# Attention on one core: normalising the last query block with a VectorE shuffle and a wide reciprocal

## Chip, cores, metric

One core of one Trainium2 chip (trn2). The metric is the time of one execution in microseconds (us) as the device reports it. The profile's span, from the first to the last instruction, is about 1.8 us shorter.

## The reference

Sixteen-head attention without mask on x of shape (1, 2048, 448), head size 28, with the QKV projection before it and the output projection after it:

```
qkv    = (x @ wqkv) reshaped to q, k, v of [B, 16, 2048, 28]
scores = einsum("bhqd,bhkd->bhqk", q, k) * 28 ** -0.5
p      = softmax(scores)
o      = einsum("bhqk,bhkd->bhqd", p, v)
out    = o (heads joined) @ wo
```

## The kernel before

Heads go in 4 groups of 4. Queries go in 4 blocks of 512. A window is one group with one block, so there are 16. In a window, the scores of each 128-key row go through an exponential, on ScalarE in tiles of 128x1024 or in a VectorE/GpSimd version, and then through PV matmuls into one PSUM bank `PO`. There each head has a strip of 32 partitions: 28 rows of unnormalised output, then row 28, the softmax denominator, because V is padded with ones. A scheduler in the kernel's Python interleaves all of this and fixes the order of instructions on each engine.

Fifteen windows get their denominators inverted in the background, by way of DMA. The last window has nothing left to hide behind. Before the change its tail was this (cut):

```python
# after key row 12 of 16: copy PO, gather the 13 rows' denominators by f32 matmuls
def partial_sums(pvop):
    ev = add(Op("DVE", 0.62, lambda: nc.vector.tensor_copy(out=OSB[...][:], in_=PO[:]), ...))
    chain_A(lambda tq: den_gather(PD[gbank[0]], ...), [ev], hold)       # lhsT = PO copy, rhs = sel
...
for j in range(NKT - NLAST, NKT):            # the last 3 key rows
    for i in range(HG):
        for tq in range(TPC):                # denominators: one-column matmuls, 48 in all
            nc.tensor.matmul(out=gb[:, col:col + 1], lhsT=pt[i][1]()[:, tq * P:(tq + 1) * P],
                             rhs=VA[g][:, 0, 0, Dh:Dh + 1], ...)
    for i in range(HG):                      # PV
        nc.tensor.matmul(out=PO[HP * st:HP * (st + 1), :], lhsT=VA[g][:, j, st, :], rhs=pt[i][1](), ...)
nc.vector.reciprocal(out=RT[:], in_=gb[:, 0:TPC * HG])      # 128 queries x 16 (4 heads x 4 tiles)
den_expand(0, nc.vector.tensor_copy); den_expand(1, nc.scalar.copy)
for hf in range(2):
    nc.vector.tensor_copy(out=OH[hf][:], in_=PO[:, hf * hw:(hf + 1) * hw])
acc(2, range(g))                             # output sums of the other three groups
for tq in range(TPC):                        # spread over the strips: f32 matmuls
    nc.tensor.matmul(out=spread[...], lhsT=RX[...], rhs=ident32[:], start=True, stop=True)
acc(3, range(g))
for hf in range(2):
    nc.vector.tensor_tensor(out=OTL[hf][:], in0=OH[hf][:], in1=spread[hf], op=ALU.mult)
    for tq in (2 * hf, 2 * hf + 1): acc(tq, (g,))
# ... two adds on VectorE, two casts on ScalarE, four output DMAs
```

The softmax here doesn't subtract the row's maximum and nothing guards it: scores larger than these inputs give would overflow.

## Time and profile before

| | before |
|---|---|
| median of 4 runs | 415.99 us (415.77 to 416.25) |
| profiled span | 414.2 us |
| ScalarE busy | 97% |
| end of the last exponential | 405.21 us |
| tail: from there to the end of the span | 9.0 us |

The page of the kernel before: the busy time of each engine, and the chain of waits followed back from the last instruction.

```profile
span 414.2 us, 7679 instructions
...
PE 366.8 (89%) x2679; PEld 124.9 (30%) x2679; DVE 395.1 (95%) x699; ACT 399.9 (97%) x439; POOL 224.9 (54%) x210
...
ACT 82%; PE 9%; issue 6%; DMA 1%; DVE 1%; SPq 0%; DVEq 0%
```

ScalarE bounds nearly the whole kernel. The 9% of TensorE does not measure the tail. Followed piece by piece (`--critical`), about 5 of these 36 us lie in the tail, 6.5 us before the first exponential and 24 us in the middle. The timeline of the tail (columns: start, duration, engine, source line, operation, output and inputs, count, idle time before it and what ended it):

```profile
403.92 1.29 ACT L934 ACTIVATE PTA_131<-PA_200 128x1024 bf16<-128x1024 f32 x1
...
404.79 0.34 PE L1069 MATMUL PD_201<-VA_110,PTA_142 128*128 128x1 bf16 x8
...
406.70 0.39 PE L1073 MATMUL PO<-PTA_131,VA_110 128*32 128x512 bf16 x2
406.80 0.26 DVE L1075 RECIPROCAL RT<-PD_201 128x16 f32<-128x16 f32 x1 [1.04 <-PE PD_201 L1069]
...
408.05 0.61 PE L1082 MATMUL PD_201<-ident_208,RX_214 128*128 128x128 f32 x4
...
408.69 0.42 DVE L1086 TENSOR_TENSOR OTL_220<-OH_211,PD_201 128x256 bf16<-128x256 f32 x1
...
409.44 0.54 PE L1062 MATMUL PA_199<-WO,OTL_220 128*128 128x448 bf16 x2
...
410.44 0.54 ACT L1093 CAST OUTF_218<-PA_199 128x448 bf16<-128x448 f32 x1
```

The last PV matmul (L1073) ends at 407.09, 1.9 us after the exponential that it needs, because TensorE still has gathers and one-column matmuls to do. VectorE's last multiply ends at 409.11. In the chain of waits of this tail, however, every piece from 402.90 to 409.99 is TensorE's, and VectorE's copies and multiplies fit in beside it. From the last PV on (start, duration, what):

```profile
407.09 0.67 PE PA_199 L1062 x3
407.76 0.44 PE PA_200 L1082 x4
408.21 0.45 PE PD_201 L1082 x4
408.65 0.57 PE PA_199 L1062 x3
```

### The profile page before, as it was taken

The numbers are of one execution on the slowest core, as the hardware profiler recorded it, in microseconds if no ns is written. First come the engines' busy times: TensorE is split into PE (matmuls) and PEld (weight loads), VectorE is DVE, ScalarE is ACT, GpSimd is POOL, SyncE is SP. The second block draws the span as 40 slices with busy tenths as digits, with TensorE's granted clock in tenths as the row PEclk, the third lists the DMA queues.
The fourth block names the chain that finished last, engine by engine and source line by source line (L and its number), as shares of the span: only waits on it lengthen the run. The fifth ranks groups of instructions, "written<-read, shape, count | busy, mean of one in ns | idle before, by whom it ended". The sixth has DMA issues, their size and how long they took to land.

```text
span 414.2 us, 7679 instructions
## 1 busy us (share of the span) xinstructions
PE 366.8 (89%) x2679; PEld 124.9 (30%) x2679; DVE 395.1 (95%) x699; ACT 399.9 (97%) x439; POOL 224.9 (54%) x210
## 2 busy tenths in 40 slices
PE   8988989898898889898897988889898988889995
PEld 5433222323232233323222222222322222222233
DVE  6899999999999999999999999999999999999974
ACT  4999999999999999999999999999999999999992
POOL 3155556474656547475555646456475656656440
PEclk9999999999999999999999999999999999999999
DMA  8410020202201011111400001010410101001012
GB/s 258 80 16 21 3 50 8 55 21 60 65 2 46 0 33 25 26 32 25 97 6 29 18 18 31 2 40 6 91 34 2 46 2 36 10 27 47 18 55 90
DMA packets 33414, 15.85 MB, mean 38 GB/s; under 512 B 26016, under 2 KB 30304, under 8 KB 33376
## 3 DMA queue, kind: packets, MB, share of 16 engines
q1 hardware_dynamic: 32304, 15.05, 14.5%
q8 instruction: 21, 0.34, 0.4%
q10 hardware_dynamic: 1072, 0.32, 0.3%
q14 instruction: 17, 0.14, 0.1%
HBM read 7.37 MB, written 1.96 MB: 23 GB/s over the span
## 4 chain that ended last, share of the span: by engine, by line
ACT 82%; PE 9%; issue 6%; DMA 1%; DVE 1%; SPq 0%; DVEq 0%
ACT PTA_131 L934 4%; ACT PTA_132 L934 4%; ACT PTA_133 L934 4%; ACT PTA_134 L934 4%; ACT PTA_145 L934 4%; ACT PTA_136 L934 4%; ACT PTA_135 L934 4%; ACT PTA_140 L934 4%; ACT PTA_144 L934 3%; ACT PTA_137 L934 3%; ACT PTA_141 L934 3%; ACT PTA_149 L934 3%; ACT PTA_148 L934 3%; ACT PTA_139 L934 3%; ACT PTA_138 L934 3%
## 5 line engine op out<-in xcount | busy, mean ns | idle before, releaser
L745 POOL TENSOR_TENSOR DG_181<-DV_175,DU_169 128x512 f16<-128x512 f16 x30 | 34.6, 1154 | 35.8 <-DVE DV_175 L742 35.6
L745 POOL TENSOR_TENSOR DG_182<-DV_176,DU_170 128x512 f16<-128x512 f16 x30 | 34.6, 1153 | 29.7 <-DVE DV_176 L742 29.1
L745 POOL TENSOR_TENSOR DG_184<-DV_178,DU_172 128x512 f16<-128x512 f16 x29 | 33.5, 1154 | 29.8 <-DVE DV_178 L742 28.5
L745 POOL TENSOR_TENSOR DG_185<-DV_179,DU_173 128x512 f16<-128x512 f16 x29 | 33.4, 1153 | 25.9 <-DVE DV_179 L742 25.8
L745 POOL TENSOR_TENSOR DG_186<-DV_180,DU_174 128x512 f16<-128x512 f16 x29 | 33.5, 1154 | 24.9 <-DVE DV_180 L742 24.7
L745 POOL TENSOR_TENSOR DG_183<-DV_177,DU_171 128x512 f16<-128x512 f16 x29 | 33.4, 1153 | 23.7 <-DVE DV_177 L742 23.6
L649 PEld LDWEIGHTS <-KB_1_94 64*128 64x128 bf16 x256 | 20.8, 93 | 48.2 <-issue 47.3
L649 PEld LDWEIGHTS <-KB_0_91 64*128 64x128 bf16 x256 | 20.5, 93 | 45.8 <-issue 42.1
L649 PEld LDWEIGHTS <-KB_1_92 64*128 64x128 bf16 x256 | 20.2, 93 | 45.8 <-issue 43.9
L649 PEld LDWEIGHTS <-KB_0_93 64*128 64x128 bf16 x256 | 20.5, 93 | 43.8 <-issue 42.7
L934 ACT ACTIVATE PTA_145<-PA_199 128x1024 bf16<-128x1024 f32 x18 | 22.6, 1254 | 0.0
L934 ACT ACTIVATE PTA_144<-PA_200 128x1024 bf16<-128x1024 f32 x18 | 22.5, 1250 | 0.0
L934 ACT ACTIVATE PTA_140<-PA_200 128x1024 bf16<-128x1024 f32 x18 | 22.5, 1249 | 0.0
L934 ACT ACTIVATE PTA_143<-PA_199 128x1024 bf16<-128x1024 f32 x18 | 22.4, 1247 | 0.0
L934 ACT ACTIVATE PTA_139<-PA_199 128x1024 bf16<-128x1024 f32 x18 | 22.4, 1246 | 0.0
L934 ACT ACTIVATE PTA_142<-PA_200 128x1024 bf16<-128x1024 f32 x18 | 22.4, 1242 | 0.0
L934 ACT ACTIVATE PTA_138<-PA_200 128x1024 bf16<-128x1024 f32 x18 | 22.3, 1241 | 0.0
L934 ACT ACTIVATE PTA_141<-PA_199 128x1024 bf16<-128x1024 f32 x18 | 22.3, 1240 | 0.0
L739 DVE TENSOR_SCALAR DU_171<-PD_203 128x512 f16<-128x512 uint16 x29 | 19.9, 685 | 1.0 <-PE PD_203 L649 0.7
L739 DVE TENSOR_SCALAR DU_172<-PD_201 128x512 f16<-128x512 uint16 x29 | 19.8, 682 | 0.9 <-PE PD_201 L649 0.9
L739 DVE TENSOR_SCALAR DU_169<-PD_201 128x512 f16<-128x512 uint16 x29 | 19.8, 684 | 0.5 <-PE PD_201 L649 0.5
L742 DVE SCALAR_TENSOR_TENSOR DV_178<-PD_201,DU_172 128x512 f16<-128x512 uint16 x29 | 19.9, 686 | 0.3
(618 smaller groups left out, 1515.5 us busy)
## 6 DMA issues: line engine op xcount, KB each, us to landing
RRB_195<-SCR_197 SPq DMA_DIRECT2D x8, 256.0 KB
RRB_196<-SCR_198 SPq DMA_DIRECT2D x7, 256.0 KB
KB_1_94<-KB_0_93 SPq DMA_DIRECT2D x4, 128.0 KB
XS_127<-in_x_dram SPq DMA_DIRECT2D x1, 448.0 KB
XS_128<-in_x_dram SPq DMA_DIRECT2D x1, 448.0 KB
XS_129<-in_x_dram SPq DMA_DIRECT2D x1, 448.0 KB
XS_130<-in_x_dram SPq DMA_DIRECT2D x1, 448.0 KB
out_dram<-XS_127 SPq DMA_DIRECT2D x1, 448.0 KB
```

The source lines that it names most:

```text
L649: nc.tensor.matmul(out=ap, lhsT=KB[g % 2][i // 2][a:a + 64, j * P:(j + 1) * P], rhs=QB[w % NQB][i // 2][a:a + 64, :], start=True, stop=Tru ...
L739: p1 = add(Op("DVE", P1, lambda: nc.vector.tensor_scalar(out=DU[b][:], in0=lo, scalar1=SIG / 65536, scalar2=SIG * (SS - 0.5), op0=ALU.mult ...
L742: p2 = add(Op("DVE", P1, lambda: nc.vector.scalar_tensor_tensor(out=DV[b][:], in0=lo, scalar=65536 * (SS - 0.5 + CE / C3), in1=DU[b][:], o ...
L745: gq = add(Op("POOL", PTT, lambda: nc.gpsimd.tensor_tensor(out=DG[b][:], in0=DV[b][:], in1=DU[b][:], op=ALU.mult), deps=[p2], prio=n, kind ...
L934: nc.scalar.activation(out=PTA[pslot.idx][:, 0:len(ns) * QW], in_=PA[s.idx][:, 0:len(ns) * QW], func=ACT.Exp, bias=ACT_BIAS, scale=ACT_SCALE)
```

## The change

The intent is to take the denominators' detour over TensorE out of the tail. A VectorE stream shuffle copies row 28 of each strip over the strip's 32 rows. A reciprocal and a multiply follow there, in two halves of 256 columns. The output sums of the other three groups are begun before the end, in whichever PSUM banks fall idle. Core of the diff (constants, set-up of `sel` and `ident32`, and the removed helpers cut):

```diff
-    SPLIT = {2: 4, 3: 2}
+    SPLIT = {2: (0, 1, 2, 3), 3: (2,)}
+    ACCQ = (0, 1, 3)
...
+    def late_sums():        # PE ops of low priority: three matmuls for each of 3 banks, once a bank is idle
+        ...
+                prev = add(Op("PE", 0.19, lambda tq=tq, gg=gg: nc.tensor.matmul(
+                    out=PD[late_acc[tq]][:, 0:D], lhsT=OT[gg][NQC - 1][:, tq * P:(tq + 1) * P], rhs=WO[:, gg, :],
+                    start=(gg == 0), stop=False), ...
...
-    for j in range(NKT - NLAST, NKT):   (one-column matmuls and PV of the last 3 rows; PV is now scheduled as usual)
-    nc.vector.reciprocal(out=RT[:], in_=gb[:, 0:TPC * HG])
-    den_expand(...) x2; tensor_copy OH x2; spread matmuls; acc(2), acc(3)
     for hf in range(2):
-        nc.vector.tensor_tensor(out=OTL[hf][:], in0=OH[hf][:], in1=spread[hf], op=ALU.mult)
+        cols = slice(hf * hw, (hf + 1) * hw)
+        nc.vector.stream_shuffle(out=DEN[hf][:], in_=PO[:, cols], mask=[Dh] * HP)
+        nc.vector.reciprocal(out=DEN[hf][:], in_=DEN[hf][:])
+        nc.vector.tensor_tensor(out=OTL[hf][:], in0=PO[:, cols], in1=DEN[hf][:], op=ALU.mult)
+        for tq in (2 * hf, 2 * hf + 1):
+            nc.tensor.matmul(out=fb[tq], lhsT=OTL[hf][:, ...], rhs=WO[:, g, :], start=(tq not in late_acc), stop=True)
...  # output tile 2 is added on VectorE, tiles 0, 1 and 3 are cast on ScalarE
```

More of the change, by code (lines that the diff above doesn't have):

```diff
@@ L108 @@
     JL = 6
+    JACC = 8
     DI = 2
-    WPE = 1
     PVM = 0.0
-    ADUR = 0.25
     PLD = 0.2
@@ L134 @@
     MG = 0.1
-    SPLIT = {2: 4, 3: 2}
+    SPLIT = {2: (0, 1, 2, 3), 3: (2,)}
+    ACCQ = (0, 1, 3)
+    ACCP = 2000
     PARTD = 60
@@ L173 @@
     DG = [sb([P, QW], F16, f"DG{i}") for i in range(NB)]
-    PARTL = [sb([P, D], F32, f"PARTL{i}") for i in range(2)]
+    PARTL = {tq: sb([P, D], F32, f"PARTL{tq}") for tq in SPLIT[NQC - 1]}
     OSB = [sb([P, QW], F32, f"OSB{i}") for i in range(2)]
@@ L189 @@
     zrow = sb([P, QW], BF16, "zrow")
-    ident32 = sb([P, P], F32, "ident32")
-    sel = sb([P, HG], F32, "sel")
-    OH = [sb([P, QW // 2], F32, f"OH{i}") for i in range(2)]
-    RT = sb([P, TPC * HG], F32, "RT")
-    RX = [sb([P, QW // 2], F32, f"RX{i}") for i in range(2)]
+    DEN = [sb([P, QW // 2], F32, f"DEN{i}") for i in range(2)]
     OUTF = [sb([P, D], BF16, f"OUTF{i}") for i in range(TPC)]
@@ L225 @@
                                 base=-(HP * i + Dh), pattern=[[0, 1]], channel_multiplier=1)
-    nc.gpsimd.memset(sel[:], 0.0)
-    for i in range(HG):
-        nc.gpsimd.affine_select(out=sel[:, i:i + 1], in_=sel[:, i:i + 1], compare_op=ALU.not_equal,
-                                fill=1.0, base=-(HP * i + Dh), pattern=[[0, 1]], channel_multiplier=1)
-    nc.gpsimd.memset(ident32[:], 0.0)
-    nc.gpsimd.affine_select(out=ident32[:], in_=ident32[:], compare_op=ALU.not_equal,
-                            fill=1.0, base=0, pattern=[[-1, P]], channel_multiplier=1)
     for g in range(G):
@@ L576 @@
     ot_done = {}
-    gbank = [None]
-    def hold(t):
-        free = [s for s in d_slots if s.free_at <= t + 1e-9]
-        if free:
-            free[0].free_at = 1e18
-            gbank[0] = free[0].idx
-        return bool(free)
     parts = {}
@@ L595, in task_part @@
         due = (12 + c) * WT - PARTD
-        for tq in range(n):
+        for tq in n:
             task = bank_task()
@@ L631 @@
     NW = G * NQC
-    NLAST = 3
-    NROW = NW * NKT - NLAST
+    NROW = NW * NKT
     rows = {}
@@ L655, in s_ready @@
                 and kmrep[(g, j // TPC, i)].done(t))
-    def chain_A(fn, deps, acq=None):
-        prev = None
-        for tq in range(TPC):
-            prev = add(Op("PE", ADUR, lambda tq=tq: fn(tq), deps=[prev] if prev else deps, prio=-5000 + tq, kind="A",
-                          lat=PLAT if tq == TPC - 1 else 0.0, acq=acq if tq == 0 else None))
-        return prev
-    def den_gather(dst, src, tqs=range(TPC)):
-        for tq in tqs:
-            nc.tensor.matmul(out=dst[:, tq * HG:(tq + 1) * HG], lhsT=src(tq), rhs=sel[:], start=(tq == 0), stop=True,
-                             skip_group_check=True)
@@ L670, in den_expand @@
-    def den_expand(hf, copy):
-        n = TPC * HG // 2
-        copy(out=RX[hf][:].rearrange("p (n e) -> p n e", e=HP),
-             in_=RT[:, hf * n:(hf + 1) * n].rearrange("p (n o) -> p n o", o=1).to_broadcast([P, n, HP]))
-    def den_spread(dst, tqs=range(TPC)):
-        for tq in tqs:
-            nc.tensor.matmul(out=dst[:, tq * P:(tq + 1) * P], lhsT=RX[tq // 2][:, (tq % 2) * P:(tq % 2 + 1) * P],
-                             rhs=ident32[:], start=True, stop=True)
-    def partial_sums(pvop):
-        ev = add(Op("DVE", 0.62, lambda: nc.vector.tensor_copy(out=OSB[(NW - 1) % 2][:], in_=PO[:]), deps=[pvop], prio=-5000))
-        chain_A(lambda tq: den_gather(PD[gbank[0]], lambda k: OSB[(NW - 1) % 2][:, k * P:(k + 1) * P], (tq,)), [ev], hold)
+    late_acc = {}
@@ new lines, in late_sums, with take, f @@
+    def late_sums():
+        def take(tq, n):
+            def f(t):
+                if pos[0] < NT - NTAIL or n and any(o.kind == "B" and o.acq is not None for o in static["PE"]):
+                    return False
+                free = [x for x in d_slots if x.free_at <= t + 1e-9]
+                if not free:
+                    return False
+                free[0].free_at = 1e18
+                late_acc[tq] = free[0].idx
+                return True
+            return f
+        prev = None
+        for n, tq in enumerate(ACCQ):
+            for gg in range(G - 1):
+                prev = add(Op("PE", 0.19, lambda tq=tq, gg=gg: nc.tensor.matmul(
+                    out=PD[late_acc[tq]][:, 0:D], lhsT=OT[gg][NQC - 1][:, tq * P:(tq + 1) * P], rhs=WO[:, gg, :],
+                    start=(gg == 0), stop=False), deps=([prev] if prev else []) + [ot_done[(g_, NQC - 1)] for g_ in range(G - 1)],
+                    prio=ACCP + tq + 0.1 * gg, kind="A", lat=0.0, acq=take(tq, n) if gg == 0 else None))
@@ L695, in finish_window @@
         ev.after = rel
-        if w >= NW - WPE:
-            ev.after = None
-            d1 = chain_A(lambda tq: den_gather(PO, lambda k: OSB[b][:, k * P:(k + 1) * P], (tq,)), [ev])
-            d2 = add(Op("DVE", 0.17, lambda: nc.vector.reciprocal(out=RT[:], in_=PO[:, 0:TPC * HG]), deps=[d1], prio=-5000))
-            d2a = [add(Op("DVE", 0.25, lambda hf=hf: den_expand(hf, nc.vector.tensor_copy), deps=[d2], prio=-5000)) for hf in range(2)]
-            d2b = chain_A(lambda tq: den_spread(PO, (tq,)), d2a)
-            d3 = add(Op("DVE", 0.62, lambda: nc.vector.tensor_tensor(out=OT[g][c][:], in0=OSB[b][:], in1=PO[:], op=ALU.mult),
-                        deps=[d2b], prio=-5000))
-            d3.after = rel
-            norm_busy[b] = d3
-            ot_done[(g, c)] = d3
-            if g == G - 2 and c in SPLIT:
-                task_part(c, SPLIT[c])
-            if g == G - 1:
-                task_OP(c)
-            return
         o1 = [add(Op("SP", 0.6, lambda: nc.sync.dma_start(
@@ L795, in fn @@
                 nc.tensor.matmul(out=PO[HP * st:HP * (st + 1), :], lhsT=VA[g][:, j, st, :], rhs=r["p"][i][1](),
-                                 start=(j == 0), stop=(j == NKT - 1 or w == NW - 1 and j == NKT - NLAST - 1),
+                                 start=(j == 0), stop=(j == NKT - 1),
                                  tile_position=(0, HP * st))
@@ L810, in aft @@
                         st_.free_at = t + SEM
-            if w == NW - 1 and j == NKT - NLAST - 1:
-                partial_sums(op)
-            if j == NKT - 1:
+            if w == NW - 1 and j == JACC:
+                late_sums()
+            if j == NKT - 1 and w < NW - 1:
                 pv_open[0] = False
@@ L1051 @@
     g = G - 1
-    last = acts[-1][2].idx
-    spare = PA[1 - last]
-    gb = PD[gbank[0]]
-    fb = [PD[k][:, 0:D] for k in range(ND) if k != gbank[0]] + [spare[:, 0:D], spare[:, QW:QW + D]]
     hw = QW // 2
-    spread = [PA[last][:, 0:hw], gb[:, hw:QW]]
-    def acc(tq, gs):
-        for gg in gs:
-            lhs = OT[gg][c][:, tq * P:(tq + 1) * P] if gg < g else OTL[tq // 2][:, (tq % 2) * P:(tq % 2 + 1) * P]
-            nc.tensor.matmul(out=fb[tq], lhsT=lhs, rhs=WO[:, gg, :], start=(gg == 0 or tq < 2), stop=(gg == g))
@@ L1064 @@
-    for j in range(NKT - NLAST, NKT):
-        pt = rows[(NW - 1, j)]["p"]
-        for i in range(HG):
-            for tq in range(TPC):
-                col = tq * HG + SI[i]
-                nc.tensor.matmul(out=gb[:, col:col + 1], lhsT=pt[i][1]()[:, tq * P:(tq + 1) * P],
-                                 rhs=VA[g][:, 0, 0, Dh:Dh + 1], start=False, stop=(j == NKT - 1), skip_group_check=True)
-        for i in range(HG):
-            st = SI[i]
-            nc.tensor.matmul(out=PO[HP * st:HP * (st + 1), :], lhsT=VA[g][:, j, st, :], rhs=pt[i][1](),
-                             start=False, stop=(j == NKT - 1), tile_position=(0, HP * st), skip_group_check=True)
@@ L1075 @@
-    nc.vector.reciprocal(out=RT[:], in_=gb[:, 0:TPC * HG])
-    den_expand(0, nc.vector.tensor_copy)
-    den_expand(1, nc.scalar.copy)
-    for hf in range(2):
-        nc.vector.tensor_copy(out=OH[hf][:], in_=PO[:, hf * hw:(hf + 1) * hw])
-    acc(2, range(g))
-    for tq in range(TPC):
-        nc.tensor.matmul(out=spread[tq // 2][:, (tq % 2) * P:(tq % 2 + 1) * P],
-                         lhsT=RX[tq // 2][:, (tq % 2) * P:(tq % 2 + 1) * P], rhs=ident32[:], start=True, stop=True)
-    acc(3, range(g))
@@ L1085 @@
-    for hf in range(2):
-        nc.vector.tensor_tensor(out=OTL[hf][:], in0=OH[hf][:], in1=spread[hf], op=ALU.mult)
-        for tq in (2 * hf, 2 * hf + 1):
-            acc(tq, (g,))
-    for tq in (0, 2, 1, 3):
-        if tq < 2:
+    fb = {tq: PD[late_acc[tq]][:, 0:D] if tq in late_acc else PA[1 - acts[-1][2].idx][:, 0:D] for tq in range(TPC)}
+    for hf in range(2):
+        cols = slice(hf * hw, (hf + 1) * hw)
[3 more added lines that the diff above has]
+        for tq in (2 * hf, 2 * hf + 1):
+            nc.tensor.matmul(out=fb[tq], lhsT=OTL[hf][:, (tq % 2) * P:(tq % 2 + 1) * P], rhs=WO[:, g, :], start=(tq not in late_acc), stop=True)
@@ L1091 @@
+    for tq in range(TPC):
+        if tq in SPLIT[c]:
             nc.vector.tensor_tensor(out=OUTF[tq][:], in0=fb[tq], in1=part(c, tq), op=ALU.add)
@@ L1093 @@
             nc.scalar.copy(out=OUTF[tq][:], in_=fb[tq])
-        (nc.scalar if tq == 3 else nc.sync).dma_start(out=out_perm[:, c * TPC + tq, :], in_=OUTF[tq][:])
+        (nc.scalar if tq == TPC - 1 else nc.sync).dma_start(out=out_perm[:, c * TPC + tq, :], in_=OUTF[tq][:])
 _INS = ['x', 'wqkv', 'wo']
```

## The prediction

> **What bounds the kernel now.** The page's busy table shows ScalarE 97% busy (399.9 of 414.2 us), and the chain of waits is 82% ScalarE exponentials. In the last stretch of the timeline the exponentials start every 0.917 us with almost no gap; the last ends at 405.21 us. The change adds and removes no exponential and moves no tile between ScalarE and VectorE/GpSimd (the instruction orders have equal counts), so only the tail after 405.21 can move much. It is 9.0 us of 414.2 (2.2%). So a change over 2% would need nearly the whole tail.
>
> **Tail before, from the timeline.** TensorE is about 1.5 us behind ScalarE: the f32 gathers (0.54 us x2 on the chain), 48 one-column matmuls (about 1.3 us) and the last PV matmuls end at 407.08. Then reciprocal 128x16 (0.257), spreading (0.29 and 0.40), copies of PO (0.42 x2), eight f32 spreading matmuls (about 0.9), partial output sums, two 0.42 us multiplies (last end 409.11), output matmuls to 409.98, ScalarE casts to 410.98, then the output DMAs to 414.2: 3.2 us after the last cast.
>
> **Removed.** All gathers, one-column matmuls, spreads, the PO copies, and the partial sums of the other groups from the tail (begun earlier in idle banks). The last PV matmul can follow the last exponential by 0.05 us and, at 0.39 us, end near 405.65 instead of 407.08. That is 1.4 us won.
>
> **Added, all serial on VectorE, twice (halves of 256 columns):** shuffle out of PSUM, reciprocal of 128x256, multiply.
> - Shuffle: [...]I cost it as the traced 128x256 f32 PSUM copy, 0.42 us.
> - Multiply: 0.42 us, traced in the same shape.
> - Reciprocal: today only 16 columns wide. The trace has 0.245 us for it, 0.157 us start to start, while a 4-column reduction occupies 0.06. The excess, about 0.095 us for 16 columns, is 5.8 ns a column against 1.04 ns for a copy (683 minus 416 ns over 256 columns). [...] Estimate for 256 columns: [...]centre 1.75 us. This is the disputed term: sixteen values per row become 512.
>
> **Sum (span time).** Shuffle 405.7 to 406.15, reciprocal to 407.95, multiply to 408.4; second half to about 411.0; two output matmuls to 411.5; cast or add to 412.1; DMA 3.2 to 415.3. So the span grows by about 1.1 us: won 1.4 us on PV and about 1.1 on gathered work after it, lost about 3.5 us in two wide reciprocals. Time 415.93 + 1.0 = 416.9 us.
>
> **Range.** [...] If its excess is a fixed cost[...] (about 0.45 us each): span about 412.6, time 414.3. I give the wide cost 85%.
>
> **What would show it.** The groups by form should show RECIPROCAL 128x256 near 1.75 us[...], not 0.42; STREAM_SHUFFLE near 0.42; the last PV end near 405.7; the chain of waits should end in VectorE, about 5 us, instead of TensorE; TensorE mostly idle after 406; the mid-kernel ScalarE pace unchanged at 0.917.
>
> **What would make it wrong.** A cheap reciprocal (faster by 1.6 us); the shuffle costing much more than a copy (mask loading); TensorE's clock falling in the idle 2 to 3 us so that the last output matmuls take twice 0.19 us; the rescheduling from the fourth-last window on making ScalarE wait once or twice (0.2 to 0.5 us).
>
> Predicted 416.9 us, range 414.2 to 418.4; faster by over 2%: 0.01, within 2%: 0.98, slower: 0.01.

The sum in this text came to a span of 415.3 us and a time of 416.9 us. The 1.75 us for each wide reciprocal is an estimate of mine: the 5.8 ns a column and about 0.15 us of overhead that the text reads from the trace make 1.63 us, and the centre was put higher by judgement.

## The result

| | before | changed |
|---|---|---|
| median of 4 runs each | 415.99 us | 417.14 us (416.94 to 417.33) |
| profiled span | 414.2 us | 415.3 us |
| end of the last exponential | 405.21 us | 405.45 us |
| tail | 9.0 us | 9.9 us |

The ratio of the fast runs is 1.0015, with a 95% interval from 0.9992 to 1.0038: the same, at 2%. The means of the listed runs give 1.0027. The two sets of four runs do not overlap.

The page of the changed kernel:

```profile
span 415.3 us, 7539 instructions
...
PE 365.1 (88%) x2617; PEld 121.4 (29%) x2617; DVE 396.9 (96%) x698; ACT 400.1 (96%) x439; POOL 223.8 (54%) x203
...
ACT 85%; issue 7%; PE 2%; DVE 2%; DMA 2%; SPq 0%; DVEq 0%
```

Again the shares of the span mix stages: late_sums below, whose tail is as long, has TensorE at 8%. Within the tail (from 404.9 us) the chain has passed from TensorE, 4.9 us before and 1.1 us now, to VectorE, none before and 5.2 us now. Its two longest pieces are the reciprocals:

```profile
406.41 1.76 DVE DEN_207 L1017
...
409.02 1.76 DVE DEN_208 L1017
```

The timeline of the changed tail, same columns:

```profile
404.17 1.28 ACT L894 ACTIVATE PTA_145<-PA_199 128x1024 bf16<-128x1024 f32 x1
...
405.50 0.39 PE L755 MATMUL PO<-PTA_145,VA_110 128*32 128x512 bf16 x2
...
405.94 0.44 DVE L1016 STREAM_SHUFFLE DEN_207<-PO 128x256 f32<-128x256 f32 x1
...
406.41 1.75 DVE L1017 RECIPROCAL DEN_207<-DEN_207 128x256 f32<-128x256 f32 x1
...
408.20 0.42 DVE L1018 TENSOR_TENSOR OTL_213<-PO,DEN_207 128x256 bf16<-128x256 f32 x1
...
409.02 1.75 DVE L1017 RECIPROCAL DEN_208<-DEN_208 128x256 f32<-128x256 f32 x1
...
410.81 0.42 DVE L1018 TENSOR_TENSOR OTL_214<-PO,DEN_208 128x256 bf16<-128x256 f32 x1
...
411.29 0.36 PE L1020 MATMUL PA_198<-WO,OTL_214 128*128 128x448 bf16 x1 [2.06 <-DVE OTL_214 L1018]
411.49 0.46 PE L1020 MATMUL PD_200<-WO,OTL_214 128*128 128x448 bf16 x1
...
411.98 0.53 ACT L1025 CAST OUTF_212<-PD_200 128x448 bf16<-128x448 f32 x1 [1.94 <-PE PD_200 L1020]
```

From these two timelines the tail can be balanced, piece by piece (ends of the named instructions, in us):

| piece | before | changed | difference |
|---|---|---|---|
| last exponential to last PV | 405.21 to 407.09: 1.88 | 405.45 to 405.89: 0.44 | -1.44 |
| last PV to last multiply | 407.09 to 409.11: 2.02 | 405.89 to 411.23: 5.34 | +3.32 |
| last multiply to last cast | 409.11 to 410.98: 1.87 | 411.23 to 412.51: 1.28 | -0.59 |
| last cast to end of span | 410.98 to 414.2: 3.2 | 412.51 to 415.3: 2.8 | -0.4 |
| sum | 9.0 | 9.9 | +0.9 |

The change won 2.0 us in the first and third pieces and paid 3.3 us in the second. The second piece is six VectorE instructions in a row, and two of them, the reciprocals, are 3.5 us of its 5.3. The 0.4 us of the last piece, the output transfers, is not shown to be a gain: this piece takes 2.9 to 3.2 us in the four profiles of the kernel before and 2.7 to 3.1 us in the nine others.

The span grew by 1.2 us (414.17 to 415.35 before rounding), 0.24 more than the tail. In the changed profile the first exponential also starts later, at 16.25 us against 16.02. The chain of waits there passes through an input transfer that landed at 9.53 us and that TensorE waited for; before, the one in the chain landed at 6.10. In all 13 traces the stretch from the first exponential's start to the last one's end is 389.2 us. So the middle of the kernel did not move, and this difference belongs to the start. In three more profiles of the unchanged kernel (below) it starts at 16.12, 16.20 and 16.49, so the start scatters by half a microsecond by itself. For that reason I compare tails below, and not spans.

### The profile page after: what moved, and what is told of

It reads as the page before. It is cut to its first block, busy times and chain, and to the rows that moved or that the text cites. A ratio compares the mean times of both kernels' runs of the same rounds, so it can differ in the third digit from the quotient of the medians.

```text
span 415.3 us, 7539 instructions
## 1 busy us (share of the span) xinstructions
PE 365.1 (88%) x2617; PEld 121.4 (29%) x2617; DVE 396.9 (96%) x698; ACT 400.1 (96%) x439; POOL 223.8 (54%) x203
## 4 chain that ended last, share of the span: by engine, by line
ACT 85%; issue 7%; PE 2%; DVE 2%; DMA 2%; SPq 0%; DVEq 0%
ACT PTA_131 L894 5%; ACT PTA_132 L894 4%; ACT PTA_133 L894 4%; ACT PTA_136 L894 4%; ACT PTA_135 L894 4%; ACT PTA_134 L894 4%; ACT PTA_145 L894 4%; ACT PTA_140 L894 4%; ACT PTA_139 L894 4%; ACT PTA_137 L894 4%; ACT PTA_138 L894 4%; ACT PTA_144 L894 4%; ACT PTA_142 L894 3%; ACT PTA_143 L894 3%; ACT PTA_141 L894 3%
## 5 line engine op out<-in xcount | busy, mean ns | idle before, releaser
L894 ACT ACTIVATE PTA_140<-PA_199 128x1024 bf16<-128x1024 f32 x18 | 22.4, 1247 | 0.0
L894 ACT ACTIVATE PTA_144<-PA_199 128x1024 bf16<-128x1024 f32 x18 | 22.4, 1245 | 0.0
L894 ACT ACTIVATE PTA_143<-PA_198 128x1024 bf16<-128x1024 f32 x18 | 22.3, 1241 | 0.0
L894 ACT ACTIVATE PTA_142<-PA_199 128x1024 bf16<-128x1024 f32 x18 | 22.3, 1239 | 0.0
L894 ACT ACTIVATE PTA_141<-PA_198 128x1024 bf16<-128x1024 f32 x18 | 22.3, 1236 | 0.0
L894 ACT ACTIVATE PTA_139<-PA_198 128x1024 bf16<-128x1024 f32 x17 | 21.1, 1241 | 0.0
L702 DVE SCALAR_TENSOR_TENSOR DV_178<-PD_200,DU_172 128x512 f16<-128x512 uint16 x29 | 19.8, 684 | 0.3
L702 DVE SCALAR_TENSOR_TENSOR DV_176<-PD_201,DU_170 128x512 f16<-128x512 uint16 x29 | 19.8, 683 | 0.2
L894 ACT ACTIVATE PTA_145<-PA_198 128x1024 bf16<-128x1024 f32 x16 | 19.9, 1247 | 0.0
```

Of the source, the lines that this page charges most:

```text
L702: p2 = add(Op("DVE", P1, lambda: nc.vector.scalar_tensor_tensor(out=DV[b][:], in0=lo, scalar=65536 * (SS - 0.5 + CE / C3), in1=DU[b][:], o ...
L894: nc.scalar.activation(out=PTA[pslot.idx][:, 0:len(ns) * QW], in_=PA[s.idx][:, 0:len(ns) * QW], func=ACT.Exp, bias=ACT_BIAS, scale=ACT_SCALE)
```

## The experiments

Theory: the two wide reciprocals, which cost by the column, lie whole on the chain of waits and turn a gain into a loss. Rivals: a fixed cost of the reciprocal, something else in the new tail (shuffle, sums, transfers), TensorE's clock falling while it idles (granted 0.90 from 410 to 412 us in the changed profile), or no gain in the other half of the change. All edits are against the changed kernel unless said otherwise. The changed kernel itself was not run again beside them; the runs of the kernel before at full clock have medians of 416.0 us. Overview (tail = end of the last exponential to end of span, in the profiled run):

| run | us, median (runs) | tail, us | correct |
|---|---|---|---|
| before, first comparison | 415.99 (4) | 9.0 | yes |
| changed | 417.14 (4) | 9.9 | yes |
| no_reciprocal | 413.59 (6) | 6.5 | no |
| pe_spread | 416.6 (6) | 9.3 | yes |
| block_transpose | 414.44 (6) | 7.2 | yes |
| ln_exp | 414.56 (6) | 7.4 | yes |
| quarters | 417.75 (1) | 10.6 | yes |
| late_sums | 417.3 (6) | 9.9 | yes |
| warm_tail | 417.26 (4) | 9.9 | yes |
| hybrid | 414.67 (6) | 7.4 | yes |

### no_reciprocal: take the suspected cost away

```diff
-        nc.vector.reciprocal(out=DEN[hf][:], in_=DEN[hf][:])
-        nc.vector.tensor_tensor(..., in1=DEN[hf][:], op=ALU.mult)
+        nc.vector.tensor_tensor(..., in1=DEN[hf][:], op=ALU.min)
```

> The changed kernel without its two 128x256 reciprocals; the multiply becomes a minimum so that the numbers stay finite. The result is wrong on purpose. Theory (the two wide reciprocals, 1.75 us each, lie whole on the chain of waits): 3.5 us less plus two short waits, about 413.5 us against 417.1 of the changed kernel, so 0.6% faster than before. Rival (the tail is held by something else, the shuffle, the output sums or the output transfers): the time falls by under 1.5 us, to 415.6 or more.

Measured: 413.59 us, 3.55 us under the changed kernel. Its output is wrong, which doesn't matter for the time. The tail is 3.4 us shorter (9.9 to 6.5). The chain of waits of its tail (start, duration, what):

```profile
405.37 0.39 PE PO L755 x2
405.76 1.24 PE PD L655 x6
407.00 0.20 PE PD L1019
```

So nearly all of the 3.5 us of the two instructions was on the chain, and the rival that something else holds the tail falls. Once the reciprocals are gone, the chain passes on to the six output-sum matmuls (L655) that stand behind the last PV, and then to three casts in a row on ScalarE (1.48 us from 407.23). This is about the floor for any cheaper inversion in this arrangement.

### quarters: fixed cost or cost by the column?

```diff
-    for hf in range(2):        # 256 columns: shuffle, reciprocal, multiply, two matmuls
+    for tq in range(TPC):      # 128 columns: shuffle, reciprocal, multiply, one matmul
```

> The changed kernel with the tail in four pieces of 128 columns. Only the form of the cost is asked. If a reciprocal costs by the column (6.29 ns from 243 ns at 16 columns and 1753 at 256), each of the four takes 0.95 us, and the span is about that of the changed kernel, at most 0.6 us more. Rival (a fixed cost that a wide or an unusual shape brings once per instruction): each takes 1.5 us or more and the span grows by 2 us or more.

Measured by the groups of instructions (busy time, then mean ns of one):

```profile
L1019 DVE RECIPROCAL DEN<-DEN 128x128 f32<-128x128 f32 x4 | 3.8, 952 | 0.1
L675 DVE RECIPROCAL DRC<-DCO 128x16 f32<-128x16 f32 x15 | 3.6, 243 | 0.0
```

From 16 to 128 columns the slope is (952 - 243) / 112 = 6.3 ns a column, and from 128 to 256 it is (1753 - 952) / 128 = 6.3 ns. It is a straight line: about 0.14 us and 6.3 ns a column. The rival of a fixed cost falls. The time, 417.75 us in one run, is 0.6 us over the changed kernel's median, the upper end of what was expected: four pieces carry the overhead of a piece four times, not twice (shuffle, reciprocal and multiply take 1.54 us at 128 columns and 2.62 at 256), and the last output matmul took 0.55 us where the three before it took 0.36 (granted clock 0.50 from 412 to 414 us). The 128x8 reciprocals of the next run fit the line too (0.18 us).

### block_transpose: the same inversion on 8 columns

A VectorE transpose of 32x32 blocks puts the denominators of 32 queries on 32 partitions of a strip, so 256 queries need 8 columns. The multiply is done in that layout, and a second transpose brings the result back.

```diff
-        nc.vector.stream_shuffle(out=DEN[hf][:], in_=PO[:, cols], mask=[Dh] * HP)
-        nc.vector.reciprocal(out=DEN[hf][:], in_=DEN[hf][:])
-        nc.vector.tensor_tensor(out=OTL[hf][:], in0=PO[:, cols], in1=DEN[hf][:], op=ALU.mult)
+        nc.vector.transpose(out=DEN[hf][:], in_=PO[:, cols])           # TN = DEN seen as 8 blocks of 32
+        nc.vector.reciprocal(out=RQ[hf], in_=TN[hf][:, :, Dh])         # 128 x 8
+        nc.vector.tensor_tensor(out=TB[hf], in0=TN[hf], in1=RQ[hf] broadcast over the block, op=ALU.mult)
+        nc.vector.transpose(out=OTL[hf][:], in_=TB[hf][:])
```

> The changed kernel with the denominators brought into 8 columns per half by VectorE 32x32 block transposes, reciprocal 128x8, multiply in the transposed layout, and a block transpose back. Six more VectorE instructions of known width (256 columns, about 0.42 us) in place of two shuffles and two wide reciprocals. Theory (a reciprocal costs about 6.3 ns a column): reciprocal 128x8 takes about 0.2 us; span near 412.5, about 414.3 us, 2.8 us under the changed kernel and 0.4% faster than before. Rival (a reciprocal costs a fixed time): each 128x8 reciprocal is above 1 us and nothing is won.

("Six more" in that text is a slip: eight VectorE instructions stand in place of six.) Measured: 414.44 us, correct, 2.7 us under the changed kernel. Its timeline between the last PV and the output matmuls:

```profile
405.88 0.78 DVE L1019 STREAM_TRANSPOSE DEN<-PO 128x256 f32<-128x256 f32 x2
406.59 0.31 DVE L1022 RECIPROCAL RQ<-DEN 128x8 f32<-128x8 f32 x2
406.82 0.39 DVE L1025 TENSOR_TENSOR TB<-DEN,RQ 128x256 bf16<-128x256 f32 x1
407.25 0.45 DVE L1027 STREAM_TRANSPOSE OTL<-TB 128x256 bf16<-128x256 bf16 x1
407.61 0.38 DVE L1025 TENSOR_TENSOR TB<-DEN,RQ 128x256 bf16<-128x256 f32 x1
...
408.03 0.45 DVE L1027 STREAM_TRANSPOSE OTL<-TB 128x256 bf16<-128x256 bf16 x1
```

Two reciprocals take 0.31 us together where they took 3.5. The same 512 values for each strip are inverted in both kernels; only the number of columns differs. The stretch from the last PV to the last normalised half is 2.6 us, against 5.3.

### ln_exp: the same values on another engine

```diff
     shuffles of both halves first, then
-        nc.vector.reciprocal(out=DEN[hf][:], in_=DEN[hf][:])
+        nc.scalar.activation(out=DEN[hf][:], in_=DEN[hf][:], func=ACT.Ln, scale=2.0 ** -40)
+        nc.scalar.activation(out=DEN[hf][:], in_=DEN[hf][:], func=ACT.Exp, scale=-1.0, bias=-40 * LN2)
     then the multiplies; the table set loaded at the start is one that has Ln and Exp
```

> The changed kernel with 1/d taken as exp(-ln d) on ScalarE, idle in the tail, between the shuffles and the multiplies; both halves are pipelined over the two engines, and the table set is one that holds both functions from the start. Theory: four ScalarE instructions of about 0.4 us in place of two of 1.75 us: last multiply near 408.3 where the changed kernel has 411.2, span near 412.3, about 414.1 us. If the other table set makes the 430 exponentials slower, the 0.917 us pace shows it and the run loses several us.

Measured: 414.56 us, correct. The four ScalarE instructions:

```profile
406.39 0.76 ACT L1018 ACTIVATE DEN<-DEN 128x256 f32<-128x256 f32 x2 [0.96 <-DVE DEN L1016]
407.06 0.70 ACT L1020 ACTIVATE DEN<-DEN 128x256 f32<-128x256 f32 x2
```

They take 1.4 us for both halves. The 389.2 us of exponentials did not change with the other table set. Two quite different replacements of the wide reciprocal give the same gain, which speaks for the reciprocal as the cause and against any effect of one particular arrangement.

### pe_spread: the other half of the change alone

The early sums and the plain PV order are kept; the denominators go over TensorE again, all of it after the last PV.

```diff
-        shuffle, reciprocal 128x256, multiply by DEN
+        copy PO to OH; 4 gathers (lhsT=OH, rhs=sel) into a free bank; reciprocal 128x16;
+        expand on VectorE and ScalarE; 4 spreads (lhsT=RX, rhs=ident32); multiply OH by the spread
```

> The changed kernel's early output sums and plain PV order, but denominators gathered and spread by TensorE with a 16-column reciprocal, all of it after the last PV. Theory: the other half of the change is a gain, only the wide reciprocals lose. Chain after the last PV: copies 0.8, gathers behind six output-sum matmuls to about 1.7, reciprocal and expansion 0.6, f32 spreads 0.9, multiply 0.4: last cast near 410.6 and span near 413.8, so about 415.5 us, 1.6 us under the changed kernel and 0.5 us under before. Rival (the early sums and the new order give nothing): 416 or more.

Measured: 416.6 us, a miss of 1.1 us, of which about 0.3 us is the later start of the profiled run (first exponential at 16.52). It is 0.5 us faster than the changed kernel, but not faster than before: the ratio is 0.9997, and it is 0.6 us over those runs of before that kept the full clock (see before_again). The trace says where my estimate was short:

```profile
407.24 0.95 PE L1031 MATMUL PA<-sel,OH 128*128 128x4 f32 x8
408.30 0.26 DVE L1033 RECIPROCAL RT<-PA 128x16 f32<-128x16 f32 x1 [1.34 <-PE PA L1031]
...
408.94 1.16 PE L1041 MATMUL PA<-ident,RX 128*128 128x128 f32 x8 [0.75 <-DVE RX L1036]
```

The gathers stand behind the six sums of the other groups, so they begin 1.0 us after the copy of PO was begun (406.20). The spreads need 1.16 us where I had 0.9, and three casts then queue on ScalarE for 1.4 us. The kernel before gathered 13 of 16 rows ahead of time; without that the route over TensorE costs as much as its removal saves. So the gain on the last PV is real (table above) but is only worth something with a cheap inversion behind it.

### late_sums: undo the early output sums

```diff
-   late_sums: matmul(out=PD[late_acc[tq]], ...) as scheduled
+   late_sums only reserves the banks; all nine matmuls are issued after the last PV
```

> The changed kernel with the early output sums undone: the three matmuls of the bank that was begun before the last PV are issued after it too, so all nine output-sum matmuls stand in the tail, about 1.75 us from 405.8. Theory: they end near 407.6, a microsecond before the first normalised half is ready, so the time does not change (417.1, within 0.2 us). Rival (the early start is part of the gain): 0.5 us or more slower.

Measured: 417.3 us against 417.14, tail 9.9 in both. In the changed kernel only three of the nine sums were in fact early. The nine stand in the timeline from 405.80 for 1.88 us, while VectorE is in its first reciprocal until 408.14:

```profile
405.80 1.88 PE L1014 MATMUL PD<-WO,OT 128*128 128x448 bf16 x9
...
406.39 1.75 DVE L1018 RECIPROCAL DEN<-DEN 128x256 f32<-128x256 f32 x1
```

The early sums are off the critical path here, hidden under the reciprocal. They would matter with a short tail: without reciprocals the remaining six already are the chain.

### warm_tail: is it TensorE's clock?

```diff
         nc.vector.reciprocal(out=DEN[hf][:], in_=DEN[hf][:])
+        for _ in range((6, 9)[hf]):
+            nc.tensor.matmul(out=<idle bank>, lhsT=zeros[:], rhs=zrow[:], start=True, stop=True)
```

> The changed kernel with six and nine dummy matmuls in an idle bank while VectorE is in the two reciprocals, so that TensorE does not idle. Theory: the granted clock between 410 and 412 us is 1.00 where the changed kernel has 0.90, the last output matmul takes about 0.35 us where it has 0.46, and the time falls by about 0.1 us, below what the clock of the runs resolves: the idle of TensorE is a small part of the loss. Rival (the falling clock is a large part): 0.5 us or more faster.

Measured: 417.26 us, no gain. First the changed kernel and then this one, in the same stretch of the tail (busy us and count of each engine, then granted clock, DMA share, GB/s):

```profile
410.00:412.00 2.00, 0.66 (x2) 0.11 (x2) 1.44 (x3) 0.07 (x2) 0.00 (x0) 0.90 0.34 115
```

```profile
410.00:412.00 2.00, 1.88 (x9) 0.60 (x7) 1.48 (x2) 0.33 (x1) 0.00 (x0) 1.00 0.34 115
```

The clock was held at 1.00, as meant, and the last output matmul took 0.35 us where it had taken 0.46. That is all there was to win, a tenth of a microsecond, below what the runs resolve. The clock is not the cause.

### hybrid: both replacements at once

First half by block transposes on VectorE, second half by shuffle and ScalarE's Ln and Exp.

```diff
+    shuffle(second half); transpose(first half)
+    ScalarE: Ln, Exp of the second half's denominators
+    VectorE: reciprocal 128x8, multiply, transpose back (first half); multiply (second half)
```

> First half of the columns by block transposes with an 8-column reciprocal on VectorE, second half by shuffle on VectorE and exp(-ln d) on ScalarE at the same time. Theory: second half ready near 408.0 where the block transposes alone have 408.5 and the ScalarE version 408.3, so 0.1 to 0.3 us under them, about 414.3 us: near the floor that the run without reciprocals shows (413.6).

Measured: 414.67 us, no better than block_transpose (414.44), so the expected 0.1 to 0.3 us did not come: the tails are 7.4 and 7.2 us. VectorE is the longer of the two arms: its instructions run almost without a gap from 406.12 to 408.39, while ScalarE's two end at 407.47. block_transpose is the version to keep. Its reported ratio to before is 0.9946 (0.9924 to 0.9968), and that ratio flatters it, as the next runs show.

### before_again: why the kernel before scattered

The kernel before was run 22 times beside the experiments. 9 of these took 417.4 to 419.1 us, at granted clocks of 0.991 to 0.996 (the text says 10, a miscount), and the other 13 took 415.7 to 416.7 us at 0.998 or more. No run of a changed version jumped like this. So the kernel before was profiled three times more, unedited.

> The unchanged kernel before, for a second profile. In the two calls before this one, 10 of its 22 runs took 416.7 to 419.1 us at a mean granted clock of 0.991 to 0.996, the others about 416 us at 1.0. Theory: in such a run TensorE's granted clock falls for one or two stretches of about 3.4 us in the middle of the kernel, each costing about 1.5 us, and the tail is as in the profile shown; a run at 416 us has no such stretch. Rival: the slower runs differ in the tail or in the input transfers. Also asked: the start of the first exponential (16.02 us in the first profile, 16.25 in that of the changed kernel), which should scatter by some tenths with the landing of the inputs.

> As before_again_1: one more draw of the same kernel, about one in three to be of the slower kind.

> As before_again_1: one more draw of the same kernel, about one in three to be of the slower kind.

They took 415.84, 417.66 and 415.94 us. The second is of the slower kind, and my theory of a dip in the middle of the kernel is wrong: the dip is in the tail. Its last windows:

```profile
404.00:406.00 2.00, 2.00 (x33) 1.34 (x32) 0.92 (x2) 1.69 (x2) 0.00 (x0) 1.00 0.00 0
406.00:408.00 2.00, 2.00 (x41) 1.18 (x40) 0.85 (x4) 0.36 (x1) 0.00 (x0) 0.64 0.47 182
408.00:410.00 2.00, 2.00 (x9) 1.60 (x8) 0.67 (x2) 0.05 (x1) 0.00 (x0) 0.50 0.15 56
410.00:412.00 2.00, 1.80 (x11) 0.89 (x10) 1.57 (x4) 0.16 (x1) 0.00 (x0) 1.00 0.00 0
```

TensorE is granted half its clock from about 406.6 to 410.0 us (0.64 over 2 us is 1.44 us at half). There the last PV, the spreads and the sums of the old tail take up to 1.8 times as long (three sums 1.30 us where the first profile has 0.74). This tail lasts 10.2 us where the first profile has 9.0. The other 0.5 us of the difference lie at the start (first exponential at 16.49). The half clock lasts 3.41 us. In the profile of the kernel before, the full clock lasts 409.60 us, from its rise at 5.41 us to a fall at 415.01, after the last instruction; in that of the changed kernel 406.19 us, from 5.42 to 411.61. These are 120 and 119 times 3.413 us, and in all 13 traces I read a whole multiple (117, 119 or 120 times, from a rise at 4.2 to 7.2 us to the first fall). Why only some runs are hit is not shown. My estimate from these lengths, which no run tests: the tail lies at another place of this 3.413 us grid in each run.

What TensorE does in a stretch of 3.413 us, counted from the rise, can be summed from the instruction records: for each matmul, the columns that it streams times the share of 128x128 that its form has (each f32 record counted twice, by choice; once or four times gives the same order). The stretch before the dip, 403.17 to 406.58, holds 2528 such columns. TensorE is shown busy for all of it, but 40 of its 52 matmuls have one or four columns. The corresponding stretch of the first profile, 401.35 to 404.77, holds 3399 (those of the other two about 3400), and no fall follows. In the changed profile the last stretch before its fall at 411.61 holds 1792, the 118 others 3200 or more. Over all 13 traces, by my count, the 14 stretches of full clock that a fall followed hold 0 to 2688 columns, and the 1536 others 2688 or more (2688 stands once on each side). For the dip itself this is a count and not an experiment; no run changed the work in that stretch, and what makes the clock fall is not shown. warm_tail is an experiment for the later fall: its dummy matmuls lift the stretch up to 413.35 to 3968 columns, and no fall follows (granted clock 1.00 from 412 to 414 us), where the changed kernel has 1792 columns and then a clock of 0.50. The slowest runs (clock 0.991, 419 us) were not caught in a profile.

So the old tail, with its one-column matmuls, met this fall in one of its four profiles. In the profiles of the changed kernel and its variants the granted clock is 1.00 up to 410 us and the fall comes only after that, when TensorE has at most the last output matmuls left; in the changed kernel it cost 0.1 us (0.46 for the last output matmul, 0.35 in warm_tail). pe_spread, also a TensorE tail but without one-column matmuls, did not jump in its six runs either. Against the runs of before at full clock (medians 416.0) the change costs 1.1 us. Against a run like the one above it is half a microsecond faster. For the same reason block_transpose beats the full-clock runs of before by 1.6 us (414.44 against 416.0, 0.4%), and not by the 0.54% of its reported ratio.

## Why the prediction was right

- **The size of the tail as the limit** (right): the exponentials keep their 389.2 us. All of the difference, apart from the scatter of the start, lies in the tail.
- **The last PV** (right): it was to end near 405.65, 1.4 us earlier. Measured from the last exponential it ends 1.44 us earlier.
- **The reciprocal** (right, and the term that decided): the forecast took 5.8 ns a column from the excess of a 16-column reciprocal over a tiny instruction, and gave 1.75 us for 256 columns. Measured: 1.753 us. The form, a cost by the column, was right (quarters); the exact hit is partly luck, since 5.8 ns a column and about 0.15 us of overhead make 1.63 us, and the centre was put higher by judgement. The measured line is 6.3 ns a column and 0.14 us. 6.3 ns is about six times the 1.04 ns of a copied column.
- **The shuffle** (right): 0.44 us against 0.42 for a copy of the shape. The mask load is a separate instruction of 14 ns. By the column it is near a copy too: 0.30 us at 128 columns (quarters) and 0.44 at 256 make 1.1 ns a column, against 1.04 ns for a copied one.
- **The sum** (right, with errors that cancel, which is luck): span 415.3 as predicted, time 417.14 against 416.9. The end after the last cast was 2.8 us and not 3.2; the last cast came 0.4 us later than forecast, of which 0.24 us were the inputs of that run and 0.1 us the clock (the last output matmul took 0.46 us, at full clock 0.35), a risk that the prediction named.
- **The output sums** (wrong, without effect): the prediction took all of them out of the tail and had TensorE mostly idle after 406. Six of the nine still stand behind the last PV and end at 407.13. It did not matter, since the first reciprocal hides them, and for the same reason the three early ones are worth nothing here (late_sums).

## What to carry to other kernels

Cost a VectorE reciprocal by its columns per partition, not by its number of values: here 6.3 ns a column, so 256 columns with every value repeated over 32 partitions cost 1.75 us where the same values in 8 columns cost 0.2. Before removing a detour to a compact layout, ask whether an expensive instruction was cheap only because of it; a 32x32 block transpose keeps the compact layout without TensorE (0.44 us for 128x256 in hybrid; 2.6 us from the last PV to the last normalised half in block_transpose). And when a kernel's runs scatter, look at the granted clock of each run and at where it falls, before a ratio of a few tenths of a per cent is believed.
